# Seven block products for eight in a three-stage kernel: attention, a gated layer, a signed layer

## The chip, the core and the metric

The kernel runs on one core of a Trainium2 chip. The metric is device time in microseconds (us). TensorE (PE; its weight loads are PEld) multiplies, VectorE (DVE), ScalarE (ACT) and GpSimd (POOL) do the rest, and transfers are issued by SyncE (SP) and, for two at the start, by ScalarE.

## What is computed

Attention over 16 heads with queries pooled in pairs, then a gated layer and a signed layer on 1152 tokens of 512 channels:

```python
q_pool = q.reshape(B, H, S // factor, factor, D).mean(axis=3)   # S 1152, D 64
scores = scale * np.matmul(q_pool, k.transpose(0, 1, 3, 2))
attn = np.exp(scores - max); attn = attn / (sum + 1e-09)
x = np.matmul(attn, v)                       # to 1152 tokens x 512
g = x @ w_gate                               # 512 x 1536
x = (g / (1 + np.exp(-g)) * (x @ w_val)) @ w_out
h = x @ w_in                                 # 512 x 2048
return (np.maximum(h, 0.0) + alpha * np.minimum(h, 0.0)) @ w_out2
```

All inputs are 32-bit floats (the scores come near to sharp maxima, since q and k are scaled up). The kernel keeps their precision by splitting every operand into a higher and a lower half and adding three products: high x high, high x low, low x high.

## The kernel before

**Order of the work.** Nothing is issued as it is written. Each step is a task (`add`) with an engine, an assumed duration, a priority, the tokens that it reads and writes, and buffers out of numbered classes; `Plan.run` (L159) walks through time and gives each engine the first task by priority that is ready and whose buffers have room, and `emit` writes the instructions down in that order. So on each engine there is one fixed order, and on the chip an instruction waits for the semaphores of its inputs. A buffer class is a set of slots in SBUF or in the eight PSUM banks; a slot is free again when all users of its buffer are done, and the buffers of one class are bound in the order in which they were asked for. The numbers in `KNOB` shift priorities (`qk`, `mn`, `exp`, ...) and set how many slots the classes have.

**Attention.** Eight pairs of heads (`p`), each on 128 partitions. Per pair: scores in `two` and `corner` (L625, L644), running minima on VectorE (`minimum`, L593 and L595), the exponential on ScalarE (L599), transposes on TensorE (L663) and their copies (L678, L679), value products (`values`, L694), and `inverses`: the row sums' reciprocals are turned (L708), written to memory (L712) and read back by three copies (L715) that spread them over partitions. `finish` (L717) multiplies the pair's output by them (L724; for the last pair L722 on VectorE) and splits it into `xh` (L727) and `xl` (L729). Pairs 0 to 3 are the first batch, 4 to 7 the second; pair `p` gives channels 128 (p mod 4) and on.

**Feed-forward.** Tokens are three blocks of 384 (`TB`), the hidden dimension is units of 128: 12 in the first layer, 16 in the second. `contract` (L780) is one unit and one block: four chunks of channels times three products, 12 matmuls (L788), into one bank. `gated` (L804) does it for a gate and a value: Silu on ScalarE (L811), the product on VectorE (L813), then `split_h` into halves (L798, L799). `prelu` (L817) is the second layer's: L827, L828, L801, L802. `out1` (L832) and `out2` (L860) multiply groups of four units by the output weights (L847, L876) and add into `part` on VectorE (L854, L884). After the last group, `out1` also splits the sum into `xh` and `xl` (L856 on GpSimd, L857). `merged` (L889) mixes a group's units with the output products of the group before; the first group takes block 0 of the first three units first, then the rest.

**Weights.** Two units at a time (for the first layer a gate and a value), `weights` (L449) loads two tiles of 512 KB, which hold the 32-bit weights inside 64-bit words, converts them with one ScalarE and three VectorE instructions of 1024 columns (L462 to L465), and splits them into a higher half (L466, ScalarE) and a lower half (L469, VectorE). The halves go to class `wc` (three slots) or, for output weights, `wr`.

## Time and profile before

| | |
|---|---|
| median of 3 runs | 641.45 us (641.05 to 641.84) |
| profiled execution | 641.22 us, its span 639.4 us |
| granted TensorE clock | 1.00 |
| TensorE busy, matmuls / weight loads | 99% / 88% |
| VectorE, ScalarE, GpSimd busy | 69%, 52%, 15% |
| attention, to the last value product | about 212 us |
| gated layer, from there | about 226 us |
| signed layer | about 198 us |

Busy times are the profile's; the matmuls are pipelined, so that one of 336 ns follows the one before by about half of that. In the rows, a matmul of the scores on unsplit floats or of the value products appears twice. A row of a timeline gives the start, the duration, the engine and the instruction, and in brackets how long the engine had been idle before it and what ended that. SPq is the queue of SyncE.

### The profile page before, as it was taken

Reading aid. Unit: us, or ns where it says so; the run is one execution under the profiler, and the core shown is the slowest. Engines: PE = TensorE matmul, PEld = TensorE weight load, DVE = VectorE, ACT = ScalarE, POOL = GpSimd, SP = SyncE. Lnnn points to the kernel's source line nnn. Section 1 sums busy time; section 2 is a strip of 40 time slices with the busy share of each in tenths; the row PEclk is TensorE's granted clock in tenths of the full one; section 3 lists DMA queues with packets and bytes.
Section 4 is the critical chain, followed back from the end, with each engine's and each line's share of the span. In section 5 each row is a group of like instructions: output and inputs, shape, how many; then the busy total and the mean of one; then the engine's idle time right before and its main releaser. Section 6 shows DMA issues by size and latency. Waiting matters only on the chain.

```text
span 639.4 us, 12152 instructions
## 1 busy us (share of the span) xinstructions
PE 633.0 (99%) x4869; PEld 565.0 (88%) x4869; DVE 441.4 (69%) x913; ACT 332.5 (52%) x554; POOL 96.2 (15%) x107
## 2 busy tenths in 40 slices
PE   8999999999999999999999999999999999999997
PEld 5777777778777899999999999999998999899986
DVE  5988788788999669857337754588887298454332
ACT  5877877787888445545334423312765464242210
POOL 5644534424212000000000000052000000000000
PEclk9999999999999999999999999999999999999999
DMA  6342132132121533433311311113124011000012
GB/s 198 100 132 89 48 127 85 48 116 84 58 86 68 150 132 133 174 120 121 114 67 66 135 65 66 67 67 132 66 73 168 23 67 66 1 1 0 1 49 100
DMA packets 17640, 55.35 MB, mean 87 GB/s; under 512 B 2792, under 2 KB 4016, under 8 KB 17584
## 3 DMA queue, kind: packets, MB, share of 16 engines
q1 hardware_dynamic: 17296, 54.19, 24.4%
q8 instruction: 38, 0.62, 0.4%
q10 hardware_dynamic: 288, 0.39, 0.2%
q14 instruction: 18, 0.15, 0.1%
HBM read 52.17 MB, written 2.40 MB: 85 GB/s over the span
## 4 chain that ended last, share of the span: by engine, by line
PE 95%; DVE 2%; issue 1%; ACT 1%; DVEq 0%
PE bank L788 39%; PE bank L876 15%; PE bank L847 12%; PE bank L694 11%; PE bank L625 8%; PE bank L663 6%; PE bank L644 2%; DVE et L679 1%; PE bank L348 1%; DVE plain L595 1%; DVE plain L698 0%; DVE plain L593 0%; ACT et L678 0%; ACT plain L599 0%; PE bank L708 0%
## 5 line engine op out<-in xcount | busy, mean ns | idle before, releaser
L788 PE MATMUL bank<-xh,weights 128*128 128x384 f32 x960 | 253.0, 336 | 0.0
L788 PEld LDWEIGHTS bank<-xh,weights 128*128 128x128 f32 x960 | 174.3, 188 | 1.8 <-issue 0.5
L788 PE MATMUL bank<-xl,weights 128*128 128x384 f32 x480 | 161.4, 336 | 0.0
L599 ACT ACTIVATE plain<-plain,stats 128x1152 f32<-128x1152 f32 x72 | 90.0, 1251 | 27.9 <-DVE plain L595 27.9
L876 PE MATMUL bank<-fed,h 128*128 128x512 f32 (+1 forms) x444 | 102.8, 384 | 0.0
L876 PEld LDWEIGHTS bank<-fed,h 128*128 128x128 f32 x444 | 81.4, 188 | 14.5
L788 PEld LDWEIGHTS bank<-xl,weights 128*128 128x128 f32 x480 | 90.2, 188 | 1.1
L595 DVE TENSOR_SCALAR_CACHE_REDUCE plain<-bank,stats 128x384 f32<-128x384 f32 x144 | 80.7, 613 | 2.1 <-PE bank L663 0.2
L847 PE MATMUL bank<-h,fed 128*128 128x384 f32 x432 | 79.0, 336 | 0.0
L847 PEld LDWEIGHTS bank<-h,fed 128*128 128x128 f32 x432 | 75.8, 188 | 0.0
L694 PE MATMUL bank<-et,plain 128*64 128x320 f32 (+1 forms) x576 | 73.4, 408 | 0.2 <-DVE et L679 0.2
L678 ACT ACTIVATE et<-bank 128x384 f32<-128x384 f32 x137 | 61.9, 489 | 12.9 <-PE bank L663 11.3
L663 PEld LDWEIGHTS bank<-ident,plain 64*128 64x128 f32 x1296 | 55.6, 138 | 14.6 <-issue 3.4
L694 PEld LDWEIGHTS bank<-et,plain 128*64 128x64 f32 x576 | 40.0, 137 | 29.4 <-DVE plain L595 2.0
L625 PE MATMUL bank<-fed 64*128 64x384 f32 x540 | 64.9, 357 | 0.2
L663 PE MATMUL bank<-ident,plain 64*128 64x64 f32 x1296 | 62.3, 231 | 1.7 <-ACT plain L599 0.6
L827 ACT ACTIVATE plain<-bank,signs 128x384 f32<-128x384 f32 x48 | 28.0, 583 | 67.8 <-PE bank L788 67.6
L828 DVE SCALAR_TENSOR_TENSOR plain<-bank,signs,plain 128x384 f32<-128x384 f32 x48 | 29.5, 615 | 37.2 <-ACT plain L827 37.0
L813 DVE TENSOR_TENSOR plain<-bank,plain 128x384 f32<-128x384 f32 x36 | 20.0, 557 | 47.5 <-PE bank L788 45.6
L625 PEld LDWEIGHTS bank<-fed 64*128 64x128 f32 x540 | 47.3, 186 | 2.8 <-DVE plain L593 1.5
L856 POOL TENSOR_SCALAR xh<-plain 128x384 fp32r<-128x384 f32 x12 | 13.3, 1111 | 205.4 <-DVE plain L854 205.4
L593 DVE TENSOR_SCALAR_CACHE_REDUCE plain<-bank 128x384 f32<-128x384 f32 x72 | 37.5, 554 | 7.0 <-PE bank L625 4.2
(70 smaller groups left out, 613.0 us busy)
## 6 DMA issues: line engine op xcount, KB each, us to landing
plain<-in_w_out SPq DMA_DIRECT2D x14, 512.0 KB, 4.1
raws<-in_w_out SPq DMA_DIRECT2D x14, 512.0 KB
plain<-in_vt SPq DMA_DIRECT2D x8, 576.0 KB, 3.9
raws<-in_w_in SPq DMA_DIRECT2D x8, 512.0 KB
plain<-in_w_in SPq DMA_DIRECT2D x8, 512.0 KB
plain<-in_qt SPq DMA_DIRECT2D x7, 576.0 KB
plain<-in_kt SPq DMA_DIRECT2D x7, 576.0 KB
raws<-in_w_gate SPq DMA_DIRECT2D x7, 512.0 KB, 5.2
```

What stands on the lines that cost most here:

```text
L593: go = lambda: nc.vector.tensor_scalar(e.ap[:, js], src(), 1.0, 3.0e38, ALU.mult, ALU.min, accum_out=m(0))
L595: go = lambda: nc.vector.tensor_scalar(e.ap[:, js], src(), 1.0, m(i - 1), ALU.mult, ALU.min, accum_out=m(i))
L599: add(ACT, act(S, True, True), lambda: nc.scalar.activation(e.ap, e.ap, AF.Exp, bias=st.ap[:, 2:3], scale=-1.0, accum_out=x.sums.ap[:, n:n ...
L625: nc.tensor.matmul(s.ap[:, j, :CUT], l(half), r(half, js), start=a == 0, stop=a == len(terms) - 1)
L663: nc.tensor.transpose(t.ap[:, j, c * D:c * D + D], e.ap[half, ks:ks + P], ident[half, half])
L678: add(ACT, act(BLK * P), lambda src=src, to=to: nc.scalar.activation(to(), src(), AF.Copy), at + turn("ev", p, n), [t], [key], [t, b], als ...
L694: nc.tensor.matmul(acc.ap[half, :n], x.vn.ap[:, (j * NK + kc) * D:(j * NK + kc) * D + D], b.ap[:, (j * BLK + c) * n:(j * BLK + c) * n + n] ...
L788: nc.tensor.matmul(acc.ap[:, :TB], l[:, cs], r[:, c, ts], start=c == 0 and a == 0, stop=c == KC - 1 and a == 2)
L827: add(ACT, act(TB) + 0.09, lambda: nc.scalar.activation(u.ap, a.ap[:, :TB], AF.Copy, scale=signs[:, 1, f:f + 1]), prio, [a, "alpha"], [u], ...
L828: add(DVE, dve(TB) + 0.056, lambda: nc.vector.scalar_tensor_tensor(u.ap, a.ap[:, :TB], sign(), u.ap, ALU.mult, ALU.max), prio, [a], [u], [ ...
L847: nc.tensor.matmul(acc.ap[:, :TB], l[:, os_], r, start=n == 0 and m == 0, stop=n == len(g) - 1 and m == 2)
L876: nc.tensor.matmul(acc.ap[:, :width], l, r[:, cols], start=n == 0 and m == 0, stop=n == len(g) - 1 and m == 2)
```

## The change

For every two units f, f+1 and the token blocks 1 and 2, the weights of the two units over the two halves of the channels form a block matrix of 2 x 2, the tokens another, and the product of the two is made with seven block products and fifteen sums in place of eight products. Token block 0 stays as it was.

- `weights` now takes two gates or two values at a time. Beside the two tiles it makes four sums of 256 columns on GpSimd (L502 of the changed kernel) and splits these, too, into a higher (L464) and a lower half (L456): a `wc` slot is twice as large, and there are two of them instead of three. Only the first two tiles are loaded during the attention, into a buffer of their own (`raw0`); the space of the others' raw tiles is shared with buffers of the attention.
- `spread` makes the seven token blocks: for each of two halves of the channels four subtractions and seven splits, on VectorE, ScalarE or GpSimd. They are made after pairs 6 and 7 for the first layer and among the last `out1` for the second. Sums 0 and 3 are B11 and B12-B11; the others need B21 or B22, which for the second half come from pair 7.
- `block` makes seven times six matmuls (`seventh`, L875), one copy on ScalarE (L892) and five additions on VectorE (`plus`, L881), and hands the four results on. Two of them are in PSUM, three sums go through SBUF; the Silu or the signed form then reads them there. `contract` (L863) is left for block 0.
- Gates of two units come before their values: `gate1`, `gate1`, `gate7`, `value1`, `value1`, `value7`.
- `finish` keeps the second and third token block unsplit (`xf`). For the last pair the multiplication is L793. The unsplit `xh`, `xl` are gone; block 0 lies in `x0`.
- At the start 34 idle products of 128 columns replace 8 of 512, and the table `KNOB` has new numbers throughout.

```diff
-    region("weights", F32R, [("wc", K["wc"], 4 * DM)])
+    region("weights", F32R, [("wc", K["wc"], 8 * DM)])
...
+        w, s = buf("wc"), buf("sum")
+        A = lambda i: mag.ap[:, 2 * P * i:2 * P * i + 2 * P]
+        U = lambda i: s.ap[:, 2 * P * i:2 * P * i + 2 * P]
+        hi = lambda i: w.ap[:, 2 * DM * i:2 * DM * i + 2 * DM]
+        lo = lambda i: w.ap[:, 4 * DM + 2 * DM * i:4 * DM + 2 * DM * i + 2 * DM]
+        for n, (a, b, op) in enumerate(((lambda: A(2), lambda: A(3), ALU.add), (lambda: U(0), lambda: A(0), ALU.subtract), (lambda: A(0), lambda: A(2), ALU.subtract), (lambda: A(1), lambda: U(1), ALU.subtract))):
+            ways = [(POOL, gp2(2 * P), lambda a=a, b=b, op=op, n=n: nc.gpsimd.tensor_tensor(U(n), a(), b(), op), True),
+                    (DVE, dve(2 * P), lambda a=a, b=b, op=op, n=n: nc.vector.tensor_tensor(U(n), a(), b(), op), True)]
+            add(prio=prio, reads=[mag] + {1: [(s, 0)], 3: [(s, 1)]}.get(n, []), writes=[(s, n)], bufs=[mag, s], **either(ways if K["sums"] else ways[:1]))
+        for i, (src, key, b) in enumerate(((lambda: mag.ap, [mag], mag), (lambda: s.ap, [(s, n) for n in range(4)], s))):
+            higher(lambda i=i: hi(i), src, 2 * DM, prio, key, [(w, i, 0)], [b, w], K["whi"])
+            lower(lambda i=i: lo(i), src, lambda i=i: hi(i), 2 * DM, prio, key + [(w, i, 0)], [(w, i, 1)], [b, w], by_pool)
+        return [(w, 0), (w, 1)]
...
+        B11, B12, B21, B22 = [lambda c=c, u=u: get(c, u) for c in (i, i + 2) for u in (0, 1)]
+        k11, k12, k21, k22 = [key(c, u) for c in (i, i + 2) for u in (0, 1)]
+        less(T, B12, B11, prio, k12 + k11, [t], held + [t])
+        split(B11, 0, k11, held, prio)
+        split(T, 3, [t], [t], prio)
+        less(T, B22, T, late, k22, [t], held + [t])
+        split(T, 4, [t], [t], late)
+        split(B22, 2, k22, held, late)
+        less(B12, B22, B12, late, k22, k12, held)
+        split(B12, 5, k12, held, late)
+        split(B21, 1, k21, held, late)
+        less(B21, B21, T, late, [t], k21, held + [t])
+        split(B21, 6, k21, held, late)
...
+        if p >= NP - 2:
+            xkey = lambda c, u: [("xf", c, 0, 0), ("xf", c, 0, 1)] if u == 0 else [("xf", c, 1)]
+            spread(lambda c, u: xf.ap[:, (c * 2 + u) * TB:(c * 2 + u + 1) * TB], xkey, [xf], x7, p - (NP - 2), at + 4.0 + K["sp"][p - (NP - 2)])
...
+    def seventh(w, xb, bank_, a, k, first, prio):
+        def go():
+            for c in range(2):
+                at = 2 * P * a + c * P
+                whi, wlo = w.ap[:, at:at + P], w.ap[:, 4 * DM + at:4 * DM + at + P]
+                for n, (l, r) in enumerate(((whi, 0), (whi, 1), (wlo, 0))):
+                    nc.tensor.matmul(bank_.ap[:, :TB], l, seven(xb, k, c, r), start=first and c == 0 and n == 0, stop=c == 1 and n == 2, skip_group_check=not first)
+        add(PE, 6 * mm(TB), go, prio, [(w, a // 4, 0), (w, a // 4, 1)] + [(xb, k, c, r) for c in range(2) for r in range(2)], [bank_], [bank_, w, of7(xb, k)])
...
+    def plus(dst, a, b, prio):
+        add(DVE, dve(TB), lambda: nc.vector.tensor_tensor(dst.ap, a.ap[:, :TB], b.ap, ALU.add), prio, [a] + ([b] if b is not dst else []), [dst], [a, b, dst])
...
+    def block(w, xb, prio, then):
+        step = lambda n: prio + n * STEP / 2
+        a = buf("b")
+        seventh(w, xb, a, 0, 0, True, step(0))
+        t0 = buf("tmp")
+        add(ACT, act(TB), lambda: nc.scalar.activation(t0.ap, a.ap[:, :TB], AF.Copy), prio, [a], [t0], [a, t0])
+        b = buf("b")
+        seventh(w, xb, b, 5, 4, True, step(1))
+        plus(t0, b, t0, prio)
+        d = buf("b")
+        seventh(w, xb, d, 6, 5, True, step(2))
+        t1 = buf("tmp")
+        plus(t1, d, t0, prio)
+        c = buf("b")
+        seventh(w, xb, c, 4, 3, True, step(3))
+        plus(t1, c, t1, prio)
+        then(1, 1, t1, True, step(3))
+        seventh(w, xb, a, 1, 1, False, step(4))
+        then(0, 0, a, False, step(4))
+        seventh(w, xb, d, 3, 6, False, step(5))
+        t2 = buf("tmp")
+        plus(t2, d, t0, prio)
+        then(1, 0, t2, True, step(5))
+        seventh(w, xb, c, 7, 2, False, step(6))
+        plus(t0, c, t0, prio)
+        then(0, 1, t0, True, step(6))
...
+    def gate7(f):
+        prio = clock[0]
+        def then(i, u, src, inside, pr):
+            bent[f, i, u] = bend(src, inside, prio)
+        block(use(("g", f))[0], x7, prio, then)
...
     for gi in range(len(g1) + 1):
-        a = [lambda f=f, tb=tb: gated(f, tb) for f, tb in sorted(((f, tb) for f in g1[gi] for tb in range(NTB)), key=lambda o: o[1] > 0 or o[0] >= K["wc"] if gi == 0 else 0)] if gi < len(g1) else []
-        b_ = [lambda o=o, tb=tb: out1(gi - 1, o, tb) for tb in range(NTB) for o in range(KC)] if gi else []
-        merged(a, b_, 0.12)
+        a, b_ = [], []
+        if gi < len(g1):
+            for f, e in pairs(g1[gi]):
+                for one, all7 in ((gate1, gate7), (value1, value7)):
+                    a += [(1.0, lambda one=one, f=f: one(f)), (1.0, lambda one=one, e=e: one(e)), (3.5, lambda all7=all7, f=f: all7(f))]
+        if gi:
+            order = [(o, tb) for tb in range(NTB) for o in range(KC)]
+            if gi == len(g1):
+                order = [(o, 0) for o in range(KC)] + [(o, tb) for i in range(2) for o in (i, i + 2) for tb in (1, 2)]
+            b_ = [(1.0, lambda o=o, tb=tb: out1(gi - 1, o, tb)) for o, tb in order]
+        merged(a, b_, K["mix1"])
...
     for gi in range(len(g2) + 1):
-        a = [lambda f=f, tb=tb: prelu(f, tb) for f in g2[gi] for tb in range(NTB)] if gi < len(g2) else []
-        b_ = [lambda tb=tb: out2(gi - 1, tb) for tb in range(NT // P)] if gi else []
+        a, b_ = [], []
+        if gi < len(g2):
+            two_ = pairs(g2[gi])
+            plain_ = [[(1.0, lambda f=f: prelu(f)), (1.0, lambda e=e: prelu(e))] for f, e in two_]
+            sevens = [[(3.5, lambda f=f: prelu7(f))] for f, _ in two_]
+            if gi == 0:
+                a = sum(plain_, []) + sum(sevens, [])
+            else:
+                a = sum((x_ + y_ for x_, y_ in zip(plain_, sevens)), [])
```

**TensorE at the end of the attention.** The last pair's transposes, value products, and what follows. `xh`/`xl` and `x0` are tokens, `fed` and `early` in L875 are the seven token blocks (in the changed kernel they lie in those regions). Before:

```order
L663 MATMUL bank<-ident,plain 128x64 x72
L708 MATMUL bank<-ident,allinv 128x64 x2
L694 MATMUL bank<-et,plain 64x320 x18
L788 MATMUL bank<-xh,weights 128x384
L788 MATMUL bank<-xl,weights 128x384
```

(L788 goes on for 336 matmuls.) With the change:

```order
L763 MATMUL bank<-turned_214,plain 64x320 x18
L863 MATMUL bank<-x_67,weights 128x384 x24
L875 MATMUL bank<-fed,weights 128x384 x18
L875 MATMUL bank<-early_3099,weights 128x384 x6
L875 MATMUL bank<-fed,weights 128x384 x6
L863 MATMUL bank<-x_67,weights 128x384 x12
L875 MATMUL bank<-early_3099,weights 128x384 x6
L875 MATMUL bank<-fed,weights 128x384 x6
L863 MATMUL bank<-x_67,weights 128x384 x12
```

Behind the value products stand 24 matmuls of block 0 where there were 72, then products on the seven blocks with single units of block 0 between them.

**SyncE at the same place.** The last pair's row sums go out (`rowd`) and come back in three copies. Before:

```order
L712 DMA rowd_111<-rows_108 9x128
L715 DMA plain<-rowd_111 64x576
L715 DMA plain<-rowd_111 64x64
L433 DMA plain<-in_w_gate 128x1024
L433 DMA plain<-in_w_val 128x1024
L433 DMA raws<-in_w_gate 128x1024
L715 DMA plain<-rowd_111 64x512
L433 DMA raws<-in_w_val 128x1024
```

With the change:

```order
L781 DMA rowd_135<-plain 9x128
L784 DMA plain<-rowd_135 64x576
L784 DMA plain<-rowd_135 64x64
L784 DMA plain<-rowd_135 64x512
L438 DMA plain<-in_w_gate 128x1024 x2
L438 DMA plain<-in_w_val 128x1024 x2
```

The third copy moved ahead of the weight loads, and the weight loads behind all of the last pair's copies.

**VectorE from the last pair's multiplication on.** L793 is that multiplication, L534 a token difference, L456 a lower half, L881 an addition of `block`. Before:

```order
L722 TENSOR_TENSOR plain<-plain 128x576
L813 TENSOR_TENSOR plain<-bank,plain 128x384
L729 TENSOR_TENSOR xl<-plain,xh 128x576
L799 TENSOR_TENSOR h<-plain,h 128x384
L464 SCALAR_TENSOR_TENSOR magnitudes<-plain,magnitudes 128x1024
```

With the change:

```order
L793 TENSOR_TENSOR plain<-plain 128x576
L534 TENSOR_TENSOR plain<-plain 128x384
L456 TENSOR_TENSOR fed<-plain,fed 128x384
L534 TENSOR_TENSOR plain<-plain 128x384
L456 TENSOR_TENSOR fed<-plain,fed 128x384
L456 TENSOR_TENSOR early_3099<-plain,early_3099 128x384
L881 TENSOR_TENSOR plain<-bank,plain 128x384
L456 TENSOR_TENSOR weights<-magnitudes,weights 128x1024
L881 TENSOR_TENSOR plain<-bank,plain 128x384 x2
L484 TENSOR_SCALAR magnitudes<-magnitudes 128x1024
L485 SCALAR_TENSOR_TENSOR magnitudes<-plain,magnitudes 128x1024
```

Token differences and their halves come first, then additions alternate with weight conversions.

## Rows read from the trace of the kernel before

**Rows 1.** The page, engines: busy us, share of the span, instructions.
```profile
PE 633.0 (99%) x4869; PEld 565.0 (88%) x4869; DVE 441.4 (69%) x913; ACT 332.5 (52%) x554; POOL 96.2 (15%) x107
```

**Rows 2.** Stretches: from:to, length, busy (count) of PE, PEld, DVE, ACT, POOL, PEclk, DMA share, GB/s.
```profile
212.00:611.40 399.40, 399.40 (x2198) 386.22 (x2197) 255.48 (x348) 167.97 (x252) 14.00 (x13) 1.00 0.23 82
212.00:270.50 58.50, 58.50 (x339) 58.45 (x338) 45.70 (x58) 30.53 (x44) 0.67 (x1) 1.00 0.43 147
437.80:469.00 31.20, 31.20 (x181) 30.95 (x180) 26.63 (x39) 21.28 (x33) 1.42 (x1) 1.00 0.24 88
```

**Rows 3.** The chain that ended last: start us, us, what.
```profile
212.12 58.44 PE bank L788 x336
...
410.76 27.07 PE bank L847 x156
...
469.22 2.72 PE bank L876 x12
```

**Rows 4.** Timelines at the seam and the end: start us, us, engine, instruction.
```profile
184.51 1.73 SPq L715 DMA_DIRECT2D plain<-rowd  x3
...
208.48 1.09 SPq L715 DMA_DIRECT2D plain<-rowd  x2
...
212.05 0.44 PE L788 MATMUL bank<-xh,weights 128*128 128x384 f32 x1
...
213.48 0.45 SPq L715 DMA_DIRECT2D plain<-rowd  x1
...
220.09 0.76 DVE L722 TENSOR_TENSOR plain<-plain 128x576 f32<-128x576 f32 x1 [0.64 <-DMA plain<-rowd]
...
636.28 0.42 DVE L884 TENSOR_TENSOR plain<-bank,plain 128x256 f32<-128x256 f32 x1 [1.01 <-PE bank L876]
```

**Rows 5.** Timeline of VectorE among the gates and, last, in the second layer.
```profile
263.97 0.69 DVE L463 TENSOR_SCALAR magnitudes<-magnitudes 128x1024 int32<-128x1024 int32 x1
264.58 1.22 DVE L469 TENSOR_TENSOR weights<-magnitudes,weights 128x1024 fp32r<-128x1024 f32 x1
265.71 1.22 DVE L464 SCALAR_TENSOR_TENSOR magnitudes<-plain,magnitudes 128x1024 int32<-128x1024 int32 x1
266.85 0.55 DVE L813 TENSOR_TENSOR plain<-bank,plain 128x384 f32<-128x384 f32 x1
267.32 1.21 DVE L465 SCALAR_TENSOR_TENSOR magnitudes<-plain,magnitudes 128x1024 int32<-128x1024 int32 x1
...
444.74 0.62 DVE L828 SCALAR_TENSOR_TENSOR plain<-bank,signs,plain 128x384 f32<-128x384 f32 x1 [0.43 <-ACT plain L827]
```

**Rows 6.** GpSimd by group (busy us, mean ns) and, first, one line (min/median/max ns).
```profile
L856 POOL TENSOR_SCALAR xh<-plain x12: 753/1118/1421, 415.6 to 438.9; 128x384 fp32r<-128x384 f32 x12
...
L724 POOL TENSOR_TENSOR plain<-plain 128x576 f32<-128x576 f32 x7 | 9.9, 1418 | 55.8 <-DVE plain L698 52.9 <-DMA plain<-rowd 2.9
L727 POOL TENSOR_SCALAR xh<-plain 128x576 fp32r<-128x576 f32 x8 | 5.4, 674 | 17.2 <-DVE plain L722 16.6
L551 POOL TENSOR_TENSOR fed<-plain,fed 128x384 fp32r<-128x384 f32 x3 | 3.0, 1000 | 3.2 <-ACT fed L549 3.1
```

**Rows 7.** Timeline at the end of the gates: two halves of a weight tile, GpSimd beside VectorE.
```profile
410.63 1.06 ACT L466 ACTIVATE weights<-magnitudes 128x1024 fp32r<-128x1024 f32 x1 [1.42 <-PE bank L788]
411.72 1.23 DVE L469 TENSOR_TENSOR weights<-magnitudes,weights 128x1024 fp32r<-128x1024 f32 x1 [0.29 <-ACT weights L466]
...
417.54 1.21 DVE L464 SCALAR_TENSOR_TENSOR magnitudes<-raws,magnitudes 128x1024 int32<-128x1024 int32 x1
417.71 1.42 POOL L856 TENSOR_SCALAR xh<-plain 128x384 fp32r<-128x384 f32 x1 [1.19 <-DVE plain L854]
```

**Rows 8.** Transfers: those of L715, and one issue group (KB each, median us to landing).
```profile
DMA to landing us min/median/max: 2.6/3.2/4.7
...
raws<-in_w_gate SPq DMA_DIRECT2D x7, 512.0 KB, 5.2
```

**Rows 9.** First scores, min/median/max ns, first and last start us.
```profile
L625 PE MATMUL bank<-plain x24: 482/483/1006, 6.1 to 11.1; 64*128 64x384 f32 x24
```

More of the change, by code (lines that the diff above doesn't have):

```diff
@@ L384, in attention_moe_moe2 @@
-    most = max(n * words for _, n, words in kinds.values())
-    def part_of(cls, i):
-        if cls not in room:
-            room[cls] = turned.tile([P, most], kinds[cls][0], name=cls, tag="turned")
-        words = kinds[cls][2]
-        return room[cls][:, i * words:(i + 1) * words]
-    for cls, (_, n, words) in kinds.items():
-        plan.place(cls, [(lambda cls=cls, i=i: part_of(cls, i), [("turned", c) for c in range(i * words // GRAIN, ((i + 1) * words - 1) // GRAIN + 1)]) for i in range(n)], ("et",) if cls == "h" else ())
@@ new lines, in attention_moe_moe2, with shared, part_of @@
+    for i in range(2):
+        bd = fed[:, 4 * S + 4 * SQ + 2 * P * i:4 * S + 4 * SQ + 2 * P * (i + 1)].rearrange("p (a t) -> p a t", a=2)
+        nc.gpsimd.memset(bd[TOP, :, LOW].bitcast(F32), 0.0)
+        nc.gpsimd.memset(bd[LOW, :, TOP].bitcast(F32), 0.0)
+    region("weights", F32R, [("wc", K["wc"], 8 * DM)])
+    def shared(name, first, then):
+        room = {}
+        most = max(sum(n * words for _, n, words in kinds) for _, kinds in (first, then))
+        def part_of(k, dt, at, words):
+            if k not in room:
+                room[k] = pools[name].tile([P, most], dt, name=f"{name}{k}", tag=name)
+            return room[k][:, at:at + words]
+        pools[name] = ctx.enter_context(tc.tile_pool(name=name, bufs=1))
+        for k, (dt, kinds) in enumerate((first, then)):
+            at = 0
+            for cls, n, words in kinds:
+                slots = []
+                for i in range(n):
+                    slots.append((lambda at=at, words=words, k=k, dt=dt: part_of(k, dt, at, words), [(name, c) for c in range(at // GRAIN, (at + words - 1) // GRAIN + 1)]))
+                    at += words
+                plan.place(cls, slots, [c for c, _, _ in first[1]] if k else ())
@@ new lines, in attention_moe_moe2 @@
+    plan.classes["e"]["slots"] += plan.classes.pop("more")["slots"]
+    for s in plan.classes["raw"]["slots"] + plan.classes["tmp"]["slots"] + plan.classes["part"]["slots"]:
+        s.after = ["e" if o == "more" else o for o in s.after]
+    at = 5 * S + 3 * SQ + 4 * P
+    zeros = plain[:, at:at + P // 2].bitcast(mybir.dt.bfloat16)
+    ident = plain[:, at + P:at + 2 * P]
+    make_identity(nc, ident)
+    nc.vector.memset(zeros, 0.0)
+    nc.gpsimd.memset(plain[:, 4 * S + 3 * SQ:4 * S + 3 * SQ + 2 * P], 1.0)
@@ L404, in attention_moe_moe2 @@
+    for i in range(K["warm"]):
+        idle(P)
+    region("magnitudes", F32, [("mag", 2, 2 * DM), ("sum", 1, 2 * DM)])
     for cls in "st":
@@ L793, in split_h @@
-    def split_h(key, tb, tmp, prio, sign=None):
-        h = hb[key]
+                at = DM * i + c * P
+                whi, wlo = w.ap[:, at:at + P], w.ap[:, 4 * DM + at:4 * DM + at + P]
+                for a, (l, r) in enumerate(((whi, 0), (whi, 1), (wlo, 0))):
+                    nc.tensor.matmul(acc.ap[:, :TB], l, x0[:, r, c], start=c == 0 and a == 0, stop=c == KC - 1 and a == 2)
+        add(PE, 3 * KC * mm(TB), go, prio, [(w, 0, 0), (w, 0, 1)] + [("x0", c, a) for c in range(KC) for a in range(2)], [acc], [acc, w])
@@ new lines, in gate7, with value7, then @@
+    def gate7(f):
[3 more added lines that the diff above has]
+        block(use(("g", f))[0], x7, prio, then)
+        clock[0] += 3.5 * STEP
+    def value7(f):
+        prio = clock[0]
+        def then(i, u, src, inside, pr):
+            sg = bent[f, i, u]
+            gate(sg, src, inside, prio)
+            split_h(("h1", f + i, u + 1), sg, prio)
+        block(use(("v", f))[0], x7, prio, then)
+        clock[0] += 3.5 * STEP
```

268 lines of the change are left out of this document (151 added, 117 removed).

## The prediction

> **What bounds the kernel now.** I read first the totals of the page: TensorE's matmuls are busy 99% of the span, its weight loads 88%, VectorE 69%, ScalarE 52%, GpSimd 15% [rows 1]. A busy TensorE proves little by itself, so the second view is the engines by stretch: from 212.0 us, where the feed-forward layers begin, to 611.4 us matmuls cover every microsecond at granted clock 1.00, while VectorE is at 64% and in its fullest stretch at 85% [rows 2]. The third view, the chain that ended last, says the same from the other side: at 212.12 us it enters a run of 336 matmuls and then passes from one group of matmuls to the next [rows 3]. So in this part a matmul removed is time removed, as long as the other engines keep up. The price of one comes from the chain, not from a matmul's own duration, since they overlap: 58.44 us for 336 is 173.9 ns; the first out-projection costs 27.07/156 = 173.5 ns, the second 2.72/12 = 226.7 ns [rows 3].
>
> **What is removed.** Each of the 20 pairs of units (6 of gates, 6 of values, 8 of the second layer) has 24 matmuls for the first token block as before, and 42 in place of 48 for the other two: 20 x 6 = 120 of 1440 matmuls of 384 columns go, 120 x 173.9 ns = **20.9 us**. All other feed-forward matmuls (432 and 444) and the attention's stay. The feed-forward then costs TensorE 1320 x 0.1739 + 432 x 0.1735 + 420 x 0.2267 + 24 x 0.12 (an estimate for half the width) = 403 us, against 424.2 from 212.05 us to the last addition at 636.28 us [rows 4]. Only the other engines can spoil this.
>
> **What is added on VectorE.** Durations are 0.55 us for 384 columns and 1.22 for 1024, but the starts of neighbours that wait for nothing lie 0.47 and 1.13 apart (0.61 for the shift of 0.69 us) [rows 5]. The signed form of 0.62 us I put at 0.53, 512 columns at 0.60, between these. Per pair of units the change adds five additions (100 x 0.47 = 47 us) and a second lower half of 1024 columns (20 x 1.13 = 23 us). In the new order I count 492 VectorE instructions from the last scaling of the attention to the closing out-projection: 315 us at these spacings, 357 us at full durations. TensorE has 403 - 30 = 373 us there (30 is the closing group: 120 wide and 24 half-wide matmuls). VectorE goes from two thirds to 84 to 96% and stays beneath TensorE. It is closest at the start: the first pair (132 matmuls, 23.0 us) has 10 additions, 10 conversions of weights and 12 others, 20.8 us at the spacings.
>
> **GpSimd** gets 80 sums of 256 columns, 76 of them in this stretch. That shape is not in the trace; two-input instructions took 1.00 us for 384 columns and 1.42 for 576 [rows 6], so I estimate 0.75. With some 20 others that moved there it is about 76 us. What it does to VectorE is the unknown. The trace shows the two in each other's way on one side: copies of 384 columns on GpSimd took 0.75 to 1.42 us, although 576 took 0.67 in the attention [rows 6], and a long one began just behind a VectorE instruction with two SBUF inputs, which kept its 1.21 us [rows 7]. So the bounds for VectorE are none and the whole 76 us; I take little, since the instruction lengthened in the rows is GpSimd's. The Trainium skill ("SBUF — State Buffer", Who interferes with whom) speaks against this change: a VectorE instruction with two SBUF inputs and a GpSimd instruction that reads SBUF exclude each other, and the later waits until the earlier is done. The trace agrees for GpSimd as the later one; by that rule VectorE would also stand behind GpSimd, which is rival 1.
>
> **ScalarE** is busy 168 of 399 us there [rows 2]; 20 new copies of half a microsecond and 20 more higher halves of 1.06 us add some 31. Weight loads (up to 5.2 us to land [rows 8]) are as many as before, and for the third tile on they start only after the last scaling, some 20 us ahead of its use. Both cost nothing under that cover; without it a tile costs its conversion, about 6 us, once.
>
> **The seam from attention to gates** holds a new wait. Before, 72 matmuls on the first token block (12.5 us) stood behind the last value product, which ended at 212.05 us [rows 4]. Now 24 stand there (4.2 us), then seven-product work. Its first product (1.04 us) needs nothing of pair 7, the second does, at 212.05 + 5.2 = 217.3 us. That sum's chain is the scaling of pair 7, one subtraction, a higher and a lower half. The scaling ran at 220.09 us, waiting for the third row copy, which was issued at 213.48 behind weight loads. Now this copy goes directly behind its two neighbours (one pair earlier the three took 1.73 us), so at about 210, and lands 2.6 to 4.7 us later [rows 4, 8]: scaling at 213 to 215. With 0.76 + 0.55 + 0.5 + 0.55 us [rows 4, 5], the 0.5 being half of the 1.06 us of 1024 columns [rows 7], and 0.1 to 0.3 per hand-over the sum is there at 215.7 to 218.3, a wait of none to 1.0 us. Later sums go through seven GpSimd instructions of 1.00 and four of 0.75, 10 us in a row, and the last is wanted some 11 us behind the start: none to 3 us. At worst, with a copy as late as before, 6 us. I take **+1.5 us**, nearest to the rows of an undisturbed copy.
>
> **Weight tiles.** The class had three slots and now has two larger ones. Once a slot was free, higher and lower half took from 410.63 to 412.95 us [rows 7]; now there are two of each, about 4.6 us, under the other slot's 66 matmuls, 11.5 us. That holds while VectorE's queue is less than 7 us behind. Such lags I put at **+1.5 us** (0 to 8).
>
> **The middle seam.** The second layer's token sums are built behind the last matmuls of the first out-projection, under 48 matmuls on the first token block (8.3 us); an addition, a subtraction and two halves are about 3 us of chain, with a queue before them: +0.5 us (0 to 2).
>
> **Attention** keeps its matmuls and, from the second pair on, TensorE's order but for one group of transposes. The head has 51 short idle products in place of 8 long and 21 short; should the first scores meet a slower TensorE, one shows 1.01 us against 0.48 [rows 9], 24 x 0.5 = 12 us at the very most and mostly under the head's own transfers. The new numbers of the table can shift waits either way: 0 (-1.5 to +2). The tail, a 0.42 us addition and a transfer [rows 4], is unchanged.
>
> **Sum.** The profiled execution took 641.22 us around its span of 639.4, 0.2 under the median of 641.45. 641.2 - 20.9 + 1.5 + 1.5 + 0.5 = 623.8, on the median's scale **624.0 us**. With every wait at its lower end 619.
>
> **The rivals.**
> 1. *VectorE stands behind GpSimd.* By my count 225 of VectorE's 321 us are forms with two SBUF inputs or the shift; seven tenths of 76 us, 53, then fall on it: 315 + 53 = 368 us against 373. No new bound, but no slack. Up to the 20th addition VectorE has 44.5 us plus seven tenths of 20 sums, 10.5, against TensorE's 52: 3 us short; with the seam at its upper end (4.5 more than I took) 631.5 us. For it: the rule above, and the first pair at 0.9. Against: no VectorE row is lengthened. 0.17.
> 2. *The seam stays open.* The copy is as late as before: 6 in place of 1.5, 628.5 us. For it: the wait of 0.64 us for just that copy [rows 4]. Against: no weight load is ahead of it any more. 0.11.
> 3. *Slower: VectorE becomes the bound.* Up to the closing group it may take 424.2 - 30 - 1 - 1 = 392 us before the gain is gone, 77 over the 315. The whole 76 us behind GpSimd gives 641 us, no change; all instructions at full duration besides (357 + 76 = 433) 682 us. It decides from half of GpSimd's time together with full durations on (38 + 42 = 80). For it: additions that each wait for the one before do run at full duration. Against: it takes both at once. 0.05, and 0.02 for no change.
> 4. That the matmuls are not removed is excluded: the new order has 480 + 840 of them.
>
> **How the numbers follow.** Forecast 0.65, rival 1 0.17, rival 2 0.11, no change 0.02, slower 0.05. The range for 8 in 10 runs from 618.5, just under no wait anywhere, to 631, which takes in rival 2 and most of rival 1. A measurement of this kernel can tell about 0.2% (1.3 us) from no change: faster by more 0.93, within it 0.02, slower 0.05.
>
> **What would show it.** Right: 1320 matmuls at 174 ns in the chain; TensorE covered from the seam on, with a gap of 1 to 3 us in its first 12 us; VectorE at 80 to 95% up to the closing group; free neighbours among the additions 0.47 us apart. Wrong: a chain that passes through VectorE or GpSimd for tens of microseconds; TensorE gaps behind lower halves at each of the 20 tiles; sums of 256 columns far over 1 us, or two-input VectorE instructions stretched beside them; an attention that ends other than near 212 us.

## The result, and the profile after

The changed kernel takes 631.22 us (631.01 to 631.42, four runs) beside 641.48 for the kernel before (641.05 to 641.84): a ratio of 0.984, interval 0.982 to 0.986. Forecast were 624.0 us and 618.5 to 631.0. The sign was right, but 10.3 of the 17.4 us came, and the time lies just above the range. The execution in the profile took 631.21 us around a span of 629.4.

The page of the changed kernel: engines (busy us, share of the span, instructions; the kernel before is in [rows 1]), then the shares of the span in the chain that ended last:

```profile
PE 617.2 (98%) x4771; PEld 547.2 (87%) x4771; DVE 527.9 (84%) x1061; ACT 369.5 (59%) x633; POOL 179.1 (28%) x200
...
PE 89%; DVE 7%; issue 2%; ACT 1%; POOL 1%; DVEq 0%; ACTq 0%; POOLq 0%
```

TensorE is still called busy, but the chain now leaves it for VectorE for 7% of the span, where it was 2% in the kernel before. The view by stretches, of TensorE alone (from:to, length, busy and number of matmuls, granted clock, DMA share, GB/s), is the one that accounts for it:

```profile
213.00:220.00 7.00, 6.24 (x36) 1.00 0.80 286
220.00:230.00 10.00, 9.36 (x50) 1.00 0.02 8
230.00:240.00 10.00, 9.54 (x55) 1.00 0.28 105
240.00:250.00 10.00, 10.00 (x59) 1.00 0.29 107
...
280.00:290.00 10.00, 9.90 (x57) 1.00 0.55 203
290.00:300.00 10.00, 8.52 (x49) 1.00 0.27 104
...
400.00:410.00 10.00, 9.22 (x52) 1.00 0.29 107
410.00:420.00 10.00, 9.26 (x53) 1.00 0.29 105
420.00:430.00 10.00, 9.76 (x57) 1.00 0.30 106
430.00:440.00 10.00, 9.61 (x52) 1.00 0.01 2
```

A full stretch of 10 us holds 59 or 60 matmuls (57.5 at 173.9 ns, and those that reach over its edges). Each one missing is 0.174 us: 3.6 us are lost from 213 to 240, 2.2 from 280 to 300, 4.1 from 400 to 440, 9.9 in all, and none in the other stretches up to 460. With an attention that ended 1.1 us later (213.12 against 212.05 [rows 4]) the sum closes: 641.2 - 20.9 + 9.9 + 1.1 = 631.3. A count can be off by one matmul at the edges of each stretch, so this is good to about 1 us. The matmuls went as counted; the prediction had 3.5 us of waits where there are 11.0.

TensorE's waits from 213 us on (instruction and line, releaser: us in total, times, longest) name two kinds:

```profile
PE bank L1006 <- DVE plain L1013: 2.0, 3, 0.9
PE bank L1006 <- ACT plain L931: 1.5, 1, 1.5
PE bank L875 <- ACT fed L464: 0.8, 1, 0.8
PE bank L875 <- POOL fed L457: 0.6, 1, 0.6
PE bank L875 <- DVE plain L936: 0.5, 1, 0.5
```

The third and fourth are token sums of the first seam. The others, 4.0 us, wait for nothing that TensorE reads: L1013, L931 and L936 are the last readers of a PSUM bank (an addition of the out-projection, a Silu, a gate). At the middle seam it looks like this (timelines of TensorE and of VectorE):

```profile
402.51 4.32 PE L1006 MATMUL bank<-turned,wide 128*128 128x384 f32 x24
407.46 2.38 PE L1006 MATMUL bank<-turned,wide 128*128 128x384 f32 x12 [0.63 <-DVE plain L1013]
410.75 19.02 PE L1006 MATMUL bank<-turned,wide 128*128 128x384 f32 x108 [0.90 <-DVE plain L1013]
```

```profile
404.59 2.35 DVE L456 TENSOR_TENSOR weights<-magnitudes,weights 128x1024 fp32r<-128x1024 f32 x2
406.86 0.55 DVE L1013 TENSOR_TENSOR plain<-bank,plain 128x384 f32<-128x384 f32 x1
407.52 1.29 DVE L456 TENSOR_TENSOR wide<-magnitudes,wide 128x512 fp32r<-128x512 f32 x2
408.74 1.49 DVE L456 TENSOR_TENSOR turned<-plain,turned 128x384 fp32r<-128x384 f32 x3
410.14 0.55 DVE L1013 TENSOR_TENSOR plain<-bank,plain 128x384 f32<-128x384 f32 x1
```

Two sums of the out-projection are done by 406.8 us. VectorE adds the first at 406.86 and, behind five halves of weights and hidden units, the second at 410.14; TensorE's next matmuls begin right behind each addition's end (407.41 and 410.69). VectorE is late, and the waits read as if a bank that it holds is the one that TensorE's next sum was given; the run with the oldest bank below tests this.

### The profile page after: what moved, and what is told of

Read it like the earlier page. It is cut to its first block, busy times and chain, and to the rows that moved or that the text cites. A ratio compares the mean times of both kernels' runs of the same rounds, so it can differ in the third digit from the quotient of the medians.

```text
span 629.4 us, 12313 instructions
## 1 busy us (share of the span) xinstructions
PE 617.2 (98%) x4771; PEld 547.2 (87%) x4771; DVE 527.9 (84%) x1061; ACT 369.5 (59%) x633; POOL 179.1 (28%) x200
## 4 chain that ended last, share of the span: by engine, by line
PE 89%; DVE 7%; issue 2%; ACT 1%; POOL 1%; DVEq 0%; ACTq 0%; POOLq 0%
PE bank L875 21%; PE bank L1040 16%; PE bank L863 12%; PE bank L763 12%; PE bank L1006 10%; PE bank L694 9%; PE bank L732 7%; PE bank L713 2%; PE bank L336 1%; DVE magnitudes L486 1%; DVE turned L748 1%; POOL magnitudes L502 1%; DVE magnitudes L485 1%; DVE wide L456 1%; DVE fed L456 1%
## 5 line engine op out<-in xcount | busy, mean ns | idle before, releaser
L502 POOL TENSOR_TENSOR magnitudes<-magnitudes 128x256 f32<-128x256 f32 x80 | 74.8, 957 | 245.7 <-DVE magnitudes L486 236.6
L875 PE MATMUL bank<-fed,weights 128*128 128x384 f32 x600 | 115.1, 336 | 1.8 <-ACT fed L464 0.8
L875 PEld LDWEIGHTS bank<-fed,weights 128*128 128x128 f32 x600 | 105.2, 188 | 3.6 <-ACT fed L464 1.1
L1040 PE MATMUL bank<-wide,turned 128*128 128x512 f32 (+1 forms) x444 | 101.7, 384 | 0.0
L1040 PEld LDWEIGHTS bank<-wide,turned 128*128 128x128 f32 x444 | 81.5, 188 | 15.6 <-DVE wide L456 0.2
L668 ACT ACTIVATE wide<-wide,stats 128x1152 f32<-128x1152 f32 x64 | 79.9, 1249 | 19.7 <-DVE wide L664 19.6
L863 PE MATMUL bank<-x,weights 128*128 128x384 f32 x480 | 88.3, 337 | 0.0
L863 PEld LDWEIGHTS bank<-x,weights 128*128 128x128 f32 x480 | 83.9, 188 | 1.3 <-issue 0.5
L1006 PE MATMUL bank<-turned,wide 128*128 128x384 f32 x432 | 78.8, 337 | 3.7 <-DVE plain L1013 2.0
L1006 PEld LDWEIGHTS bank<-turned,wide 128*128 128x128 f32 x432 | 75.0, 188 | 5.8 <-DVE plain L1013 3.4
L881 DVE TENSOR_TENSOR plain<-bank,plain 128x384 f32<-128x384 f32 x100 | 55.3, 553 | 15.5 <-PE bank L875 11.7
L464 ACT ACTIVATE weights<-magnitudes 128x1024 fp32r<-128x1024 f32 x40 | 41.7, 1055 | 32.3 <-POOL magnitudes L502 12.6
L456 DVE TENSOR_TENSOR weights<-magnitudes,weights 128x1024 fp32r<-128x1024 f32 x38 | 47.8, 1273 | 4.7 <-ACT weights L464 4.6
L875 PE MATMUL bank<-early,weights 128*128 128x384 f32 x240 | 48.7, 337 | 0.0
```

Of the source, the lines that this page charges most:

```text
L456: ways = [(DVE, dve(w), lambda: nc.vector.tensor_tensor(dst(), src(), hi().bitcast(F32), ALU.subtract), True), (POOL, gp2(w), lambda: nc.g ...
L502: ways = [(POOL, gp2(2 * P), lambda a=a, b=b, op=op, n=n: nc.gpsimd.tensor_tensor(U(n), a(), b(), op), True), (DVE, dve(2 * P), lambda a=a ...
L668: add(ACT, act(S, True, True), lambda: nc.scalar.activation(e.ap, e.ap, AF.Exp, bias=st.ap[:, 2:3], scale=-1.0, accum_out=x.sums.ap[:, n:n ...
L863: nc.tensor.matmul(acc.ap[:, :TB], l, x0[:, r, c], start=c == 0 and a == 0, stop=c == KC - 1 and a == 2)
L875: nc.tensor.matmul(bank_.ap[:, :TB], l, seven(xb, k, c, r), start=first and c == 0 and n == 0, stop=c == 1 and n == 2, skip_group_check=no ...
L1006: nc.tensor.matmul(acc.ap[:, :TB], l[:, os_], r, start=n == 0 and m == 0, stop=n == len(g) - 1 and m == 2)
```

## The experiments

Three theories stood at the start. **L**: VectorE stands behind GpSimd's sums (rival 1 of the prediction). **V**: VectorE's own work is late. **C**: the seams' chains of token sums are too long. **B**, that the *choice* of the bank is at fault, came out of the waits above and the first four runs. In all the changed kernel's 631.2 us is the yardstick, and every engine's order stayed as it was in all but the two versions with values first and the run that moves the sums to VectorE, where they stand in its queue. The kernels with narrow sums of weight blocks or narrow block sums at the first seam also fill a region with a constant at the start, on GpSimd.

**Narrow sums of weight blocks.**

```
-nc.gpsimd.tensor_tensor(U(n), a(), b(), op)
+nc.gpsimd.tensor_tensor(U(n)[:, :16], a()[:, :16], b()[:, :16], op)
```

> The 80 sums of weight blocks on GpSimd work on 16 of their 256 columns, in the same places of every engine's order (the rest of the three products that use them works on a constant put into the buffer once at the start). The kernel with the change takes 631.2 us; by the matmul counts of stretches of 10 us it loses 9.9 us in the feed-forward layers, 3.6 of them between 213 and 240 us, 2.2 between 280 and 300, 4.1 between 400 and 440. Theory L: these are lost because VectorE's instructions with two SBUF inputs stand behind GpSimd's sums (and the second weight half behind their end): without the sums 5 to 8 us come back, 623 to 626 us, and VectorE's 38 lower halves of 1024 columns fall from 1273 ns to 1220. Theory V: VectorE's own work is what is late there: at most 1.5 us come back, 629.7 to 631.2 us.

Measured: 628.50 us (627.34 to 629.08), 2.7 back: between the two. The stretch from 290 to 300 us is full again (59 matmuls), that from 400 to 410 is not (47). VectorE's lower halves of 1024 columns fell from 1273 to 1230 ns.

**Narrow additions.**

```
-nc.vector.tensor_tensor(dst.ap, a.ap[:, :TB], b.ap, ALU.add)
+nc.vector.tensor_tensor(dst.ap[:, :32], a.ap[:, :32], b.ap[:, :32], ALU.add)
```

> The 100 additions of block products on VectorE work on 32 of their 384 columns, same order on every engine (the rest of those tiles keeps what it held). That takes some 0.35 us from each, 35 us of VectorE, and leaves GpSimd's sums alone. Theory V (VectorE's own work is late around the three lossy stretches): 4 to 7 us come back, 624 to 627 us. Theory L (it stands behind GpSimd's sums): 0 to 3 us, 628 to 631 us.

Measured: 628.42 us (627.92 to 628.76), 2.8 back. Taking 36 us of work from VectorE (its additions fall from 553 to 188 ns) gives no more than taking 54 from GpSimd, and 400 to 410 stays open here too (50 matmuls). That is in L's range, but the narrow sums fell short of L as well: neither theory holds alone.

**Sums on VectorE.**

```
-nc.gpsimd.tensor_tensor(U(n), a(), b(), op)
+nc.vector.tensor_tensor(U(n), a(), b(), op)
```

> The 80 sums run on VectorE in place of GpSimd, each where GpSimd's start stood in the order: VectorE has about 80 x 0.34 = 27 us more to do, and GpSimd none of its 74.8 us of sums to stand in VectorE's way. Theory L: the lock costs more than the sums, 626 to 631 us. Theory V: VectorE falls behind further in the fullest stretches, 633 to 640 us.

Measured: 633.11 us (632.70 to 634.38), at the lower edge of V's range. This run also shows what the sums on GpSimd cost VectorE. Groups of VectorE (busy us, mean ns), in the changed kernel and then with GpSimd's sums gone:

```profile
L881 DVE TENSOR_TENSOR plain<-bank,plain 128x384 f32<-128x384 f32 x100 | 55.3, 553 | 15.5 <-PE bank L875 11.7 <-ACT turned L922 0.9
L456 DVE TENSOR_TENSOR weights<-magnitudes,weights 128x1024 fp32r<-128x1024 f32 x38 | 47.8, 1273 | 4.7 <-ACT weights L464 4.6
L456 DVE TENSOR_TENSOR turned<-plain,turned 128x384 fp32r<-128x384 f32 x36 | 23.4, 678 | 1.0 <-ACT turned L464 0.6
```

```profile
L881 DVE TENSOR_TENSOR plain<-bank,plain 128x384 f32<-128x384 f32 x100 | 55.3, 553 | 11.4 <-PE bank L875 8.1 <-ACT turned L922 0.9
L456 DVE TENSOR_TENSOR weights<-magnitudes,weights 128x1024 fp32r<-128x1024 f32 x38 | 46.5, 1239 | 1.8 <-ACT weights L464 1.8
L456 DVE TENSOR_TENSOR turned<-plain,turned 128x384 fp32r<-128x384 f32 x36 | 19.2, 553 | 0.7 <-ACT turned L464 0.2
```

With two SBUF inputs VectorE's instructions are longer beside GpSimd (678 against 553 ns); with one input in PSUM (L881) they are not. The two groups lose 1.3 + 4.2 = 5.5 us, where the prediction's bounds were 0 and 76. In the changed kernel's trace the 13 instructions of the third group that overlap one of GpSimd took 899 ns on the mean, the other 23 took 552. The 5.5 us are less than the sums cost when VectorE does them itself (80 of 418 ns, 33.1 us).

**Sums done twice.**

```
-nc.gpsimd.tensor_tensor(U(n), a(), b(), op)
+[nc.gpsimd.tensor_tensor(U(n), a(), b(), op) for _ in range(2)]
```

> Each of the 80 sums on GpSimd is done twice in a row, with the same result: some 60 to 75 us more on GpSimd, and each second weight half about 3 us later. Theory L: what the sums cost is paid again, 5 to 8 us, 636 to 639 us. Theory V: 631 to 633 us.

Measured: 685.46 us (683.54 to 688.23), 54 us more: far outside both. VectorE's waits there:

```profile
DVE weights L456 <- ACT weights L464: 39.4, 15, 4.7
```

The second lower half of a weight tile stands at the head of VectorE's queue until ScalarE's higher half comes, which waits for the sums, and everything behind it, the additions that give banks back included, stands too. In the changed kernel the same row reads 4.6 us in seven waits. The time holds a slower clock as well: its four executions had a mean granted clock of 0.965 to 0.977, those of the changed kernel 0.996 to 1.000, and in the trace six matmuls right behind a wait of 3.71 us took 2.29 us, six behind one of 1.09 us took 1.30. How the 54 us divide between waits and clock, no run shows.

**Narrow block sums at the first seam**, in `spread`, for pair 7 only (halves of the first five blocks, all subtractions).

```
-higher(lambda: seven(xb, k, i, 0), src, TB, ...
+higher(lambda: seven(xb, k, i, 0)[:, :wide(k)], lambda: src()[:, :wide(k)], TB, ...
```

> At the seam from attention to gates, the block sums of the two middle-pair token blocks that wait for pair 7 (seven of the fourteen) work on 32 of 384 columns in their subtractions, and in the higher and lower halves of five of the seven (the columns left out hold what was there); order as in the changed kernel. Between 213 and 240 us that kernel loses 3.6 us by its matmul counts. Theory C (the chain scaling, subtraction, higher half, lower half of these sums is too long for its cover of 24 matmuls): 1.5 to 3 us come back, 628.2 to 629.7 us. Theory W (the weight tile of the first values and its lower halves are late there, the token sums only stand beside it): under 0.7 us, 630.5 to 631.2.

Measured: 627.92 us (627.79 to 628.16), 3.3 back, more than C asked for. From 220 to 230 us there are 60 matmuls for 50.

**Narrow block sums at the middle seam**, the same for the second layer's fourteen, every half and subtraction on 32 columns.

> At the middle seam all fourteen block sums of the second layer's tokens work on 32 of 384 columns, in subtractions, higher and lower halves (the rest keeps the first layer's values); order as in the changed kernel. 4.1 us are lost between 400 and 440 us. Theory C (these sums are late): 1.5 to 2.5 us come back, those of 420 to 440, 628.7 to 629.7 us. Theory B (TensorE waits there for PSUM banks that a VectorE addition at the end of a queue gives back): the 1.9 us between 400 and 420 stay in both theories, and the later ones too, 630.5 to 631.2 us.

Measured: 629.32 us (628.88 to 630.17), 1.9 back, in C's range. From 420 to 440 the stretches fill (60 and 59); from 400 to 410 there are 48. That does not speak against the banks: with the oldest bank (next run) the stretches from 420 to 440 are as full with these sums at their whole width, so here too the sums cost through the banks.

**The oldest free bank.** The planner took the first free bank of its list, and that is the one given back last whenever the others are held or lie behind it. Now:

```
-        for s in c["slots"]:
+        for s in sorted(c["slots"], key=lambda s: s.since if b.cls in OLDEST else 0.0):
...
-                    b.slot.buf = None
+                    b.slot.buf, b.slot.since = None, now
```

> The planner gives each new sum in PSUM the free bank that has been free longest, in place of the first free one in its list; the order on every engine stays as in the changed kernel, row by row. In that kernel's trace TensorE's visible waits for something other than token sums (4.0 us in five waits) are all for an instruction that reads a bank for the last time (the additions of the out-projection, a Silu, a gate). Theory B (the wait is for this very bank, and another bank was free): 2.5 to 5 us come back, 626 to 629 us. Theory V or L (all banks are taken because VectorE is late): 0 to 0.7 us, 630.5 to 631.2 us.

Measured: 625.24 us (624.68 to 625.72), **6.0 back**, with every instruction in its place and no work taken away. From the first matmul behind the attention to the last one, the profiled executions took 412.8 us in the changed kernel and 407.2 with the rule; their attentions ended at 213.12 and 212.15 us. TensorE's waits, then its timeline at the middle seam and VectorE's:

```profile
PE bank L875 <- ACT fed L464: 0.8, 1, 0.8
PE bank L875 <- POOL fed L457: 0.6, 1, 0.6
PE bank L875 <- DVE plain L881: 0.3, 1, 0.3
PE bank L1006 <- DVE wide L456: 0.2, 1, 0.2
```

```profile
399.14 5.54 PE L1006 MATMUL bank<-turned,wide 128*128 128x384 f32 x31
404.92 24.11 PE L1006 MATMUL bank<-turned,wide 128*128 128x384 f32 x137 [0.25 <-DVE wide L456]
```

```profile
401.21 2.35 DVE L456 TENSOR_TENSOR weights<-magnitudes,weights 128x1024 fp32r<-128x1024 f32 x2
403.49 0.55 DVE L1013 TENSOR_TENSOR plain<-bank,plain 128x384 f32<-128x384 f32 x1
404.18 1.29 DVE L456 TENSOR_TENSOR wide<-magnitudes,wide 128x512 fp32r<-128x512 f32 x2
405.39 1.49 DVE L456 TENSOR_TENSOR turned<-plain,turned 128x384 fp32r<-128x384 f32 x3
406.80 0.55 DVE L1013 TENSOR_TENSOR plain<-bank,plain 128x384 f32<-128x384 f32 x1
```

VectorE does the same in the same time: its second addition lies 3.31 us behind the first, against 3.28 in the changed kernel. TensorE no longer minds: its next sum goes into the bank that has been free longest. The waits for a bank's last reader are gone, and those for token sums stay as they were. The 0.3 us for L881 are inside a `block`, whose sixth product adds to the very bank that L881 reads.

**The oldest of other buffers too**, with `OLDEST` holding six classes in place of one.

> As the run before, and the same rule for the temporary tiles, the tiles of hidden units, raw weights, magnitudes and output weights; same order on every engine. Theory B, if other buffers bind as well: 1 us or more below the run with banks alone. If only banks bind: within 0.5 us of it.

Measured: 625.01 us (624.93 to 626.35), within 0.5 us: of these six classes only the banks bind.

**The kernel before with the oldest bank**, the same edit.

> The kernel before, with the rule that a new sum in PSUM takes the bank that has been free longest; its order stays row by row on every engine. Theory B as stated so far (the change took VectorE's slack, and with it the chosen bank became binding): the kernel before had slack, so nothing or little moves, 640.8 to 641.8 us, and 16 us of the 641.5 are then the change's own. If the rule is worth as much in the kernel before (635 to 637 us), the missing gain was never the banks'.

Measured: 641.24 us (640.98 to 641.85) beside 641.53, a ratio of 0.9996 (0.9986 to 1.0006). Nothing: before, VectorE gave banks back early enough for either choice. With the rule in both kernels the change is worth 16.0 us (641.24 to 625.24).

**Oldest bank and narrow sums.**

> The rule of the oldest bank together with the sums of weight blocks on 16 of 256 columns (the products that use them work on a constant beside). The rule alone gave 625.2 us, the narrow sums alone 2.7 of the 6.0. If the sums cost only through the bound banks: 624.4 to 625.4 us. If VectorE's waits behind GpSimd have a price of their own: a further 2 to 3 us, 622 to 623.5 us.

Measured: 624.77 us (624.25 to 625.00), 0.5 below the rule alone. Most of the sums' 2.7 us was paid through the banks.

**Oldest bank and sums twice.**

> The rule of the oldest bank together with the sums done twice. With the first free bank the doubled sums cost 54 us (685.5), and VectorE stood 39.4 us at the head of its queue before lower halves of weights, for ScalarE's higher half behind the sums. Theory B: with free banks a tile's delay is caught in part by the other banks, 640 to 665 us. If the delay of the tile itself is what TensorE waits for (both slots of weights taken), the rule changes little: 675 to 686 us.

Measured: 672.74 us (671.38 to 673.62), 13 of the 54 us back, between the two and just outside the second. VectorE waits at its queue's head as before (40.8 us), and these are the largest waits of TensorE:

```profile
PE bank L875 <- ACT plain L892: 16.2, 5, 6.2
PE bank L875 <- DVE plain L881: 10.5, 6, 5.2
```

Neither theory has them. All eleven are for a bank inside one `block`: its fifth, sixth or seventh product adds to a bank that holds an earlier product, and L892 or L881 must have read that first. In the longest wait, 6.17 us, the copy L892 stands in ScalarE's queue behind a higher half that waits for the sums. A choice among free banks cannot help there, since the bank is fixed. No wait is for a tile of `weights`; one of 2.8 us is for output weights. Here too the granted clock was lower (0.971 to 0.980).

**Values first**, a version: in the first pair

```
+a += both[0][:2] + both[1][:2] + both[0][2:] + both[1][2:] if f == 0 else both[0] + both[1]
```

where `both` holds the gates' and the values' two plain products and their seven block products; for this order eight numbers of the table are set anew: `hold_pe=0.005, floor=34.073, sp=(-0.539, -0.622), hold_act=0.343, hold_dve=0.206, hold_pool=0.726, lead=3.144`.

> A version on what the runs showed: the rule of the oldest bank, and in the first pair of units the plain products of the values stand with those of the gates ahead of the seven block products, so that 48 matmuls of the first token block in place of 24 cover the token sums of pair 7; nine numbers of the table are set anew for this order. The rule alone has 625.2 us and still loses some 2 to 2.5 us between 213 and 230 us. Theory C: 1 to 2.5 us come back, 622.5 to 624.5 us. If the seam's wait only moves on (the second weight slot is held longer, the third tile starts later): 625 to 627 us.

Measured: 625.37 us (624.97 to 625.99). The seam's two waits are gone, but twelve of those matmuls now run inside the attention, whose last value products begin at 211.33 us in place of 207.16, with a new wait of 0.6 us for a Silu. That is 4.2 us later, where twelve matmuls are 2.1: the gain is spent there.

**The same order with the table left alone.**

> The rule of the oldest bank, the first pair's plain products of values ahead of its seven block products (48 matmuls of cover in place of 24), and the table of numbers as in the changed kernel, so that the attention keeps its order up to the last value products. Theory C: the seam's 2 to 2.5 us shrink to under 1, 623 to 624.5 us. If the wait moves to the next weight tile, whose slot is held 24 matmuls (4.2 us) longer: 625 to 627 us.

Measured: 625.95 us (625.45 to 626.02). The 48 matmuls run without a gap from 212.62 to 221.21, and the loss comes up further on:

```profile
PE bank L875 <- DVE plain L881: 1.2, 2, 0.7
PE bank L1006 <- ACT wide L464: 0.6, 1, 0.6
...
PE bank L1006 <- DVE wide L456: 0.5, 2, 0.3
```

TensorE now waits for an addition inside a block (L881, at 227 and 289 us) and for output weights (L464 and L456 into `wide`), and from 280 to 290 us there are 47 matmuls. The wait moved in part to another tile's conversion, though not to the one expected.

**Oldest bank and narrow block sums at the first seam.**

> The rule of the oldest bank together with the narrow block sums of pair 7 at the first seam (32 of 384 columns, as in the run with those alone). The rule alone gave 625.2 us, the narrow sums alone 627.9 (3.3 us less than the changed kernel). Theory C (what is left at the first seam is those sums): the two add up but for what both removed, 622.5 to 624 us. If the seam's wait is by then the weights' or the banks' alone: 624.8 to 625.4 us.

Measured: 623.21 us (622.67 to 623.86), 2.0 below the rule alone, as C has it: of what the rule leaves at the first seam, 2.0 us are pair 7's token sums.

## Why the prediction was wrong

**What is removed.** Right: 120 matmuls at 173.9 ns, and outside the three places every stretch is full.

**The sum lacked a term: the PSUM banks.** The step that failed is the one from "VectorE goes from two thirds to 84 to 96% and stays beneath TensorE" to the price of its lag: it was to cost TensorE only through a weight tile, nothing "while VectorE's queue is less than 7 us behind" (+1.5 us), and at the middle seam (+0.5). The banks were put at nothing without a reason. VectorE did stay beneath TensorE (busy 344 of the 398 us from 213 to 611, 86%). But a TensorE whose next sum is given a bank that VectorE still has to read waits for a queue that is only 2 to 3 us behind (rows at 406.86 and 410.14), and no term had that. It costs 6.0 us: the rule of the oldest bank returns them with the order unchanged, and it is worth nothing in the kernel before, which had the same eight banks and the same way of choosing. With it the kernel takes 625.2 us, 1.2 above the forecast, and the waits left in the three places are 3.9 us by the counts of matmuls, where the three terms were 3.5, though they are spread otherwise (below).

The Trainium skill ("Perfetto Trace Analysis", Matmuls) asks that independent matmul groups go round through different PSUM banks, so that emptying one overlaps the next group's matmuls. The runs agree, with 6.0 us beside it. No row of the kernel before could show a bank given too soon, but the code could: the search for a free bank begins at the head of its list each time.

**GpSimd, and rival 1.** The price of a sum was low on the mean: 957 ns for 0.75. Half of the 80 took 746 ns or less, the longest 1807. Beside VectorE instructions with an input in PSUM, four took 2.98 us:

```profile
251.83 2.98 POOL L502 TENSOR_TENSOR magnitudes<-magnitudes 128x256 f32<-128x256 f32 x4 [6.98 <-DVE magnitudes L486]
```

The rule that the prediction weighed (the Trainium skill, "SBUF — State Buffer", Who interferes with whom) has VectorE wait as the later one too. The trace agrees, with 678 against 553 ns. "I take little" was right in size, 5.5 us of VectorE for the two groups and not seven tenths of 76. Rival 1 named 631.5 us, which is what came, but by another way: without the sums 2.7 us come back, and with banks that don't bind 0.5. That its number fits is luck.

**The seam from attention to gates.** +1.5 (0 to 6) forecast, 3.6 us in the changed kernel. With the oldest bank 2.7 are left by the counts (31 matmuls from 213 to 220 us, 55 from 220 to 230), 2.0 of them pair 7's token sums by the last run. Rival 2 is refuted: pair 7's multiplication ran at 213.87 us, inside the forecast 213 to 215. What the token sums wait for is a queue, ScalarE's (its timeline):

```profile
217.58 0.49 ACT L931 ACTIVATE plain<-bank 128x384 f32<-128x384 f32 x1 [1.59 <-PE bank L863]
217.97 1.05 ACT L464 ACTIVATE weights<-magnitudes 128x1024 fp32r<-128x1024 f32 x1
218.92 1.34 ACT L464 ACTIVATE fed<-plain 128x384 fp32r<-128x384 f32 x3
```

The first difference of tokens was there at 215.64 us (VectorE, L534), but its higher half stands behind a Silu, for which ScalarE waits 1.59 us on TensorE, and behind a higher half of weights. VectorE's lower half then waits 3.8 us, TensorE 0.8.

**The middle seam and the weight tiles.** 4.1 and 2.2 us in place of 0.5 and 1.5. With the oldest bank 0.6 (56 of 59.5 matmuls from 400 to 410, all full behind it) and 0.6 (from 280 to 300) are left; the one wait that shows there is 0.35 us for an addition inside a block, not for a weight tile.

**Attention.** Its end came at 213.12 us, but that is in part the execution: with the narrow block sums at the middle seam, whose attention is the same, it came at 212.42. The term of 0 (-1.5 to +2) stands.

**ScalarE and loads** at nothing: right for the loads. ScalarE's order shows at the first seam and, through a bank, in the longest single wait of the changed kernel, 1.5 us for a Silu. The tail was as forecast.

## What to carry to other kernels

When a change takes the slack of the engine that empties PSUM, ask not only whether it still keeps up on the mean, but which buffer the waiting engine is given next: an average of 85% leaves peaks several us late, and in this kernel the first-free choice handed them on where the longest-free one absorbed them, at no cost in instructions. In a trace such a wait shows as one for an instruction whose result the waiting one does not read. Where a product adds to a bank that another engine must read first, the choice did not help. Count matmuls by equal stretches to close a sum: losses too small to be gaps show there, and they say where to look.

## What was not expected of the hardware

TensorE's clock fell early in the profiled execution of the changed kernel, not between layers. After idle times of 0.58, 0.27 and 0.25 us in the first exponentials, nine score products took 3.06 us:

```profile
12.12 0.83 PE L732 MATMUL bank<-plain,wide 64*128 64x64 f32 x13 [0.58 <-ACT wide L668]
13.21 1.59 PE L732 MATMUL bank<-plain,wide 64*128 64x64 f32 x23 [0.27 <-DVE wide L664]
15.05 3.06 PE L713 MATMUL bank<-fed 128*128 128x384 f32 x9 [0.25 <-DVE wide L664]
```

By stretches the granted clock from 15 to 18 us is

```profile
15.00:18.00 3.00, 2.95 (x9) 0.54 0.55 184
```

near 0.50, the lower level of 1.2 GHz; ahead of it 1.00 was granted. It cost little here: the one run of the same kernel with a mean clock of 1.000 took 631.01 us, the others, at 0.996 to 0.997, 631.21 to 631.42. With the oldest bank it was more: 624.68 and 624.89 us at 1.000 and 0.999, 625.59 and 625.72 at 0.997; where the clock fell in the last two is not recorded. In the run with six classes the profiled execution shows it at the first seam, behind waits of 0.76 and 1.06 us (220 to 230 us, TensorE):

```profile
220.00:230.00 10.00, 9.34 (x45) 0.83 0.01 2
```

That execution took 626.35 us, the other three of the kernel 624.93 to 625.07, with a mean clock of 0.999 to 1.000.
